# Sending the last quarter's stack rows from the middle of their section, and planning one weight chunk's loads four units later

## The chip, the cores and the metric

The kernel runs on one core of a Trainium2 chip. The core has five engines with a program each: PE (TensorE: matmuls, and its weight loads, shown as PEld), DVE (VectorE), ACT (ScalarE), POOL (GpSimd) and SP (SyncE, which here only issues DMAs). An engine works through its own program in order; engines wait for each other, and for DMAs, on semaphores. The metric is the device time of one execution in microseconds (us), lower is better.

## The reference

The sequence has 2048 rows of 512 numbers. A gate `g` (a sigmoid of a weighted row sum) mixes two results: a two-dimensional Fourier transform written as matrix products, and softmax attention with 32 heads of 16 dimensions.

```python
x = A_x
g = _sigmoid((x * gate_w).sum(-1, keepdims=True))
a = _A_ref(x, ...)     # Real((Cr + i*Ci) @ (x @ Dre.T + i * x @ Dim.T))
...
scores = jnp.einsum("bhqd,bhkd->bhqk", q, k) * scale
p = _softmax(scores, axis=-1)
o = jnp.einsum("bhqk,bhkd->bhqd", p, v)
return g * a + (1 - g) * b     # b = o @ wo
```

Everything is fp32. Products that need it are made from a rounded high part and a low part of each operand (three matmuls instead of one).

## The kernel before

**Attention.** The heads are taken as 16 pairs. The work on the values is cut in 512 *units*, 32 for each pair; `valued` counts the units done. In a unit PE makes score tiles (line 738: a stack `ks` of the keys times a stack `qs` of the queries, 128 keys x 512 queries), ACT takes their exponentials into `pt` (line 739), and PE multiplies `pt` by the values `vt` (line 774, for the last 16 units line 755). In the last 16 units (496 to 511, all of the last pair) the work goes by quarters of 512 queries: units 496 to 503 are the third quarter, 504 to 511 the last.

**Maxima and stack rows.** The exponent needs each query's maximum subtracted. So for every pair, ahead of its scores, PE makes the scores a second time with queries on the partitions (`a_tile`, line 223) and DVE takes their maxima into `mx` (line 225). When a block of queries is through, two functions are put on a list, `deferred`. The first, `m_parts`, folds and negates the maxima on DVE (line 236, `nm`) and splits them into a high and a low part on POOL (lines 239 and 240, `nhl`). The second, `m_rows`, transposes these on DVE (line 244, `mt`) and sends them by eight small DMAs (line 248) into two rows of each head's query stack `qs`: four issued by SP for the first head of the pair, four by POOL for the second. These are the *stack rows*. A score of line 738 reads them as two further rows of its contraction, so it can't start before they are there. For the last pair's second half a block is a quarter, 512 queries.

**What sets the order.** The order is written out. `segment` goes through a pattern of slots: "s" is a score, "a" a tile for the maxima, and each is set beside one matmul of a chain on the other half of the array (line 429; here the product of the attention's output with `wo`). "d" is such a matmul alone. "^" runs one function of `deferred` if there is one. "|" ends the section: first `run_plan` runs what is planned for that unit, then `values` takes two units. One further function of `deferred` is run behind the "|". Each section of the last stretch is named below by its `valued`, 496, 498, 500 and so on, and has its own pair of units behind its scores; scores run two units or more ahead of the values, so the last quarter's first scores stand in section 502.

**The plan.** `at(u, f)` enters a function for unit u; `run_plan` runs all that stand up to `valued + 1`, in order of u and then of entry. For unit 500 stand, in this order: `inverse` for the last four pairs of the first half of the queries (line 534: reciprocal of the softmax sums `rc` on DVE; line 539: two DMAs to `r` in DRAM), `last_block` step 0 (lines 552 and 553: four loads into `o_raw` of 256 KB each, the unscaled output and the reciprocals spread over the rows), and `load_w15` (line 649: eight loads of 64 KB, the chunk of `wo` for the last pair). Step 1 of `last_block` (unit 503, line 587) multiplies the two on POOL, step 2 (unit 505, lines 575 and 576) splits the product on DVE into `o_l`. The chunk w15 is read by the last pair's own products (line 691), first in section 510.

**The end of a quarter.** `LastPair` turns a quarter's finished sum: `copy` (line 666), `turn` (line 672: PE adds and transposes; lines 674 and 676: DVE divides by the sums), `back` (line 682), `products` (line 691). `finish` (line 609) adds a chain's result into an output row block `yp` on DVE; chains use PSUM banks that the scores use too, so a late `finish` or `turn` holds up the next score in that bank.

A DMA that SP issues also waits, if need be, until an earlier DMA with the same semaphore has landed; eight semaphores go round.

Of the kernel before, what the change touches and what calls it, by code (L numbers as in the profile page):

```python
# [32 lines left out]
def mix_kernel(ctx: ExitStack, tc: tile.TileContext, xa_t, xa, wqkv, w_hid, w_seq, wo, gate_w, out):  # L33
# [577 lines left out]
    def proj(hf, cts, pools, qts=range(8), whole=True):  # L611

        for n, qt in enumerate(qts):
            t = hf * 8 + qt
            chain = Chain(pools[n % len(pools)], 3 * len(cts))
            for ct in cts:
                h1, l1 = oh[hf, ct][qt]
                for i, (st, mv) in enumerate(((h1, 0), (h1, 1), (l1, 0))):
                    last = ct == cts[-1] and i == 2
                    yield chain, st, wos[0][:, mv, ct], partial(proj_next, hf, cts, t, chain, whole) if last else None  # L620
# [177 lines left out]
    def take(gen, n, whole=True):  # L798

        got = []  # L800
        while len(got) < n:
            x = next(gen, None)
            if x is None:
                break
            x[0].left -= 1
            got.append((*x, x[0].left == 0))
            if whole and got[-1][4]:
                break
        return got
# [24 lines left out]
    def at(u, f, *args):  # L834
        plan.setdefault(u, []).append(partial(f, *args))
# [19 lines left out]
        at(u, last_block, step, 1, 3, nc.gpsimd)  # L855
    for step, u in enumerate((500, 503, 505)):
        at(u, last_block, step, 0, 4, nc.gpsimd)
    at(500, load_w15)
    lead = a_next

    def run_plan(u):
# [47 lines left out]
    def segment(pattern, half, ds, stop, between=None, hold=True):  # L909


        nonlocal now
        nonlocal users
        before, users = users, []
        ds, late = iter(ds), []
        back = late if hold else None
        for n, slot in enumerate(pattern.split()):
            if slot == "|":
                for f in late:
                    f()  # L920
                add_sums()
                run_plan(valued)
                if between:
                    between()
                values()
                continue
            if slot == "^":
                if deferred:
                    deferred.pop(0)()
                continue  # L930
            now += 1
            ahead = pattern == FULL and 0 < n < 15
            if ahead:
                score(slot[0], 1 - half)
            if len(slot) == 1:
                x = next(ds, None)
                if x:

                    before = before if x[0].begun else None
                    i = issue(x, half, stop, back)  # L940
                    users = []
                    if before:
                        tc.add_manual_dep(
                            i.ins, dict(before[::-1]).get("s", before[0][1]).ins.name,
                            mybir.DependencyInfo(mybir.DependencyClass.Sync, mybir.DependencyReason.DATA))
                        before = None
            if not ahead and slot != "d":
                score(slot[0], 1 - half)
            if len(slot) == 2:
                score(slot[1].lower(), half)  # L950
        if deferred:
            deferred.pop(0)()
# [40 lines left out]
    for hf, qts in ((1, range(2)), (1, range(2, 5)), (1, range(5, 8)), (0, range(2))):  # L993
        for half in range(2):
            ds = take(proj(hf, (3,), [held_bank] * (len(qts) - 1) + one, qts, half == 1), 9, False)
            if valued < UNITS - 12:
                pattern = TEN[half]
            else:
                pattern = "s s s s s s s s |" if len(qts) < 3 else "s s s s d s s s s |"
                if valued == UNITS - 2:  # L1000
                    pattern = "s s s s d d |"
            segment(pattern, half, ds, True, after.get(valued), False)
# [38 lines left out]
```

## Time and profile before

| what | us |
|---|---|
| median of 3 runs (1694.8 to 1695.85) | 1694.96 |
| the profiled execution | 1694.88 |
| its span, first to last instruction | 1693.1 |
| PE busy in it | 1672.5 (99%) |
| DVE, ACT, POOL busy | 1375.7, 1246.4, 751.0 |
| chain that ended last: share of PE | 97% |

The profile of one execution gives the busy time of each engine, the waits (who waited for whom: total, times, longest), the chain of work that ended last, followed back from the end, a timeline of instructions with start and duration, and for any stretch the busy times and the TensorE clock that was granted, as a share of full speed. Times within the span count from its first instruction. PE is busy nearly all of the time, so what can be won lies in the few stretches in which it isn't.

### The profile page before, as it was taken

How to read it: one execution, taken by the hardware profiler on the slowest of the kernel's cores; microseconds unless marked ns; L12 is line 12 of the kernel's file. 1: busy time of each engine (PE TensorE's matmuls, PEld its weight loads, DVE VectorE, ACT ScalarE, POOL GpSimd, SP SyncE). 2: the span in 40 equal slices, each digit the busy share in tenths (PEclk: the TensorE clock that was granted, in tenths of full speed). 3: DMA queues.
4: the chain of work that ended last, by engine and by line, in shares of the span. 5: the costliest groups of instructions: out<-in, count | busy, mean ns of one | idle time of the engine just before them, and what ended most of it. 6: DMA issues, size and time to landing. Idle time of an engine off the chain costs nothing.

```text
span 1693.1 us, 34606 instructions
## 1 busy us (share of the span) xinstructions
PE 1672.5 (99%) x13120; PEld 1016.5 (60%) x13120; DVE 1375.7 (81%) x2295; ACT 1246.4 (74%) x2471; POOL 751.0 (44%) x814
## 2 busy tenths in 40 slices
PE   9999999999999999999999999999999999999987
PEld 7888766655555555555555555555555555555543
DVE  5448688888888888888888888888888888889864
ACT  5212288887777788788877887887787888888874
POOL 0114634554444465454444565545544565222331
PEclk9999999999999999999999999999999999999998
DMA  9963501314141533314164534342231636540122
GB/s 301 332 151 119 170 8 23 44 56 76 38 83 46 102 102 82 73 43 88 45 145 175 115 108 97 80 76 63 70 71 45 128 98 154 218 70 8 36 58 105
DMA packets 82622, 165.16 MB, mean 98 GB/s; under 512 B 19904, under 2 KB 20168, under 8 KB 78616
## 3 DMA queue, kind: packets, MB, share of 16 engines
q1 hardware_dynamic: 77832, 162.30, 37.0%
q8 instruction: 103, 1.69, 0.5%
q0 software_dynamic: 4480, 0.39, 0.3%
q14 instruction: 63, 0.52, 0.1%
q10 hardware_dynamic: 144, 0.26, 0.0%
HBM read 107.73 MB, written 54.52 MB: 96 GB/s over the span
## 4 chain that ended last, share of the span: by engine, by line
PE 97%; DMA 1%; DVE 1%; POOL 1%; issue 0%; SPq 0%; ACT 0%; DVEq 0%; POOLq 0%; ACTq 0%
PE d L429 39%; PE t L774 27%; PE t L223 12%; PE t L738 7%; PE t L318 4%; PE t L90 2%; PE t L91 2%; PE t L89 2%; PE t L336 1%; PE t L755 1%; PE t L429 1%; DVE mx L225 0%; DMA w<-wo 0%; DMA raw<-wqkv 0%; POOL hl L295 0%
## 5 line engine op out<-in xcount | busy, mean ns | idle before, releaser
L225 DVE TENSOR_REDUCE mx<-t 128x1 f32<-128x512 f32 x2022 | 1254.9, 683 | 211.2 <-PE t L223 171.6
L739 ACT ACTIVATE pt<-t 128x512 f32<-128x512 f32 x2048 | 1034.2, 629 | 23.4 <-PE t L738 12.9
L738 PE MATMUL t<-qs,ks 50*128 50x512 f32 x2048 | 741.8, 410 | 11.3 <-DMA qs<-mt 10.7
L223 PE MATMUL t<-ks,qs 48*128 48x512 f32 x2022 | 690.3, 400 | 0.1
L429 PE MATMUL d<-xab,ch 64*128 64x512 f32 x2016 | 656.8, 400 | 0.0
L774 PE MATMUL t<-pt,vt 128*32 128x512 f32 x3968 | 477.1, 598 | 0.2
L429 PEld LDWEIGHTS d<-xab,ch 64*128 64x128 f32 x2016 | 357.8, 184 | 132.5 <-issue 98.9
L738 PEld LDWEIGHTS t<-qs,ks 50*128 50x128 f32 x2048 | 371.1, 185 | 78.1 <-DVE mx L225 38.0
L223 PEld LDWEIGHTS t<-ks,qs 48*128 48x128 f32 x2022 | 367.7, 186 | 80.7 <-ACT pt L739 41.2
L429 PE MATMUL d<-xab,cl 64*128 64x512 f32 x1008 | 403.7, 400 | 0.0
L789 POOL TENSOR_TENSOR osum<-osum,oe 128x512 f32<-128x512 f32 x217 | 279.3, 1287 | 161.8 <-ACT oe L783 159.1
L783 ACT COPY oe<-t 128x512 f32<-128x512 f32 x217 | 127.5, 588 | 230.7 <-PE t L774 228.2
L774 PEld LDWEIGHTS t<-pt,vt 128*32 128x32 f32 x3968 | 103.9, 109 | 231.0 <-issue 148.4
L374 POOL CAST ch<-craw 128x512 fp32r<-128x512 f32 x126 | 77.3, 613 | 351.1 <-PE t L738 300.4
L429 PEld LDWEIGHTS d<-xab,cl 64*128 64x128 f32 x1008 | 185.7, 184 | 67.6 <-issue 51.1
L375 POOL TENSOR_TENSOR cl<-craw,ch 128x512 fp32r<-128x512 f32 x126 | 162.4, 1288 | 10.2
L248 POOL DMA_DIRECT2D qs<-mt x132 | 74.1, 567 | 82.2 <-DVE mt L244 77.2
L429 PE MATMUL d<-wo_hl,o_hl 64*128 64x512 f32 x288 | 77.4, 395 | 0.0
L429 PE MATMUL d<-wre,xab 64*128 64x512 f32 x288 | 70.4, 389 | 0.0
L429 PEld LDWEIGHTS d<-wo_hl,o_hl 64*128 64x128 f32 x288 | 52.2, 185 | 14.0 <-DVE yp L609 5.0
L429 PEld LDWEIGHTS d<-wre,xab 64*128 64x128 f32 x288 | 52.9, 185 | 4.1 <-DVE mx L225 0.3
L90 PE MATMUL t<-xab,wh 128*128 128x512 f32 x128 | 49.9, 390 | 0.2 <-DVE xab L86 0.2
(121 smaller groups left out, 915.4 us busy)
## 6 DMA issues: line engine op xcount, KB each, us to landing
craw<-w_seq SPq DMA_DIRECT2D x128, 256.0 KB
qk<-hl SPq DMA_DIRECT2D x32, 512.0 KB
qs<-qk SPq DMA_DIRECT2D x96, 128.0 KB
ks<-qk SPq DMA_DIRECT2D x96, 128.0 KB
b<-hl SPq DMA_DIRECT2D x16, 512.0 KB
xab<-b SPq DMA_DIRECT2D x16, 512.0 KB
o<-osum SPq DMA_DIRECT2D x62, 128.0 KB
oh<-nh SPq DMA_DIRECT2D x12, 512.0 KB
```

What stands on the lines that cost most here:

```text
L90: nc.tensor.matmul(ps, sh, ml, start=False, stop=False)
L223: nc.tensor.matmul(ps, qs[p % 2][r, qt * P:(qt + 1) * P], ks[p % 2][r, kb * 512:(kb + 1) * 512], start=True, stop=True)
L225: user = nc.vector.tensor_reduce(mx[p % 2][:, h, qt, kb:kb + 1], ps, AX.X, ALU.max)
L248: (nc.sync, nc.gpsimd)[h].dma_start(rows.rearrange("v (q b c) -> v b q c", q=n, b=4)[:, b], mt[k % 2][32 * b + h:32 * b + 4 * n:2])
L374: nc.gpsimd.tensor_copy(h1, raw)
L375: nc.gpsimd.tensor_tensor(l1, raw, h1.bitcast(F32), ALU.subtract)
L429: i = nc.tensor.matmul(self.ps, st[r], mv[r], start=not self.begun, stop=stop)
L738: nc.tensor.matmul(ps, ks[p % 2][rr, kt * P:(kt + 1) * P], qs[p % 2][rr, q0:q0 + 512], start=True, stop=True)
L739: return nc.scalar.activation(pts[u][:, 2 * qb + h], ps, AF.Exp, bias=0.0, scale=DH ** -0.5)
L774: nc.tensor.matmul(acc[32 * j:32 * j + 32], vt[:, kt, p, h:h + 32], pt[:, j], start=u == us[0], stop=u == us[-1])
L783: nc.scalar.copy(oe, acc)
L789: nc.gpsimd.tensor_tensor(o, o, oe, ALU.add)
```

## The change

Two lines differ. The sections from `valued` 500 on get a "^" behind their second score, which runs one function of `deferred` there rather than behind the section's end. And `load_w15` is entered for unit 504 instead of 500.

```diff
     for step, u in enumerate((500, 503, 505)):
         at(u, last_block, step, 0, 4, nc.gpsimd)
-    at(500, load_w15)
+    at(504, load_w15)
...
             else:
-                pattern = "s s s s s s s s |" if len(qts) < 3 else "s s s s d s s s s |"
+                pattern = "s s ^ s s s s s s |" if len(qts) < 3 else "s s ^ s s d s s s s |"
                 if valued == UNITS - 2:
                     pattern = "s s s s d d |"
```

Only one function is on the list in these sections: `m_rows` of the last quarter, in section 500. On DVE, this is the piece of the program in that section, before (-) and with the change (+); `nhl` is what POOL split, the three line 609 are the section's finishes, line 534 is the reciprocal of `inverse`:

```order
 L236 TENSOR_REDUCE nm_170<-mx_168 128x2x4
+L244 STREAM_TRANSPOSE mt_174<-nhl_172 128x32
 L609 SCALAR_TENSOR_TENSOR yp_20655<-t,omg,yp_20655 128x512
 L609 SCALAR_TENSOR_TENSOR yp_20656<-t,omg,yp_20656 128x512
 L609 SCALAR_TENSOR_TENSOR yp_20657<-d,omg,yp_20657 128x512
 L534 RECIPROCAL rc<-rc 128x64
-L244 STREAM_TRANSPOSE mt_174<-nhl_172 128x32
 L609 SCALAR_TENSOR_TENSOR yp_20655<-t,omg,yp_20655 128x512
```

The transpose has moved ahead of three finishes and the reciprocal; nothing else on DVE has moved.

On SP, the program at the same place before the change; `w` is the chunk w15, line 528 loads the softmax sums, line 627 is the first output row block:

```order
 L528 DMA rc<-o_104 64x1x64 x2
 L539 DMA r_151<-rc 16x4x64 x2
 L552 DMA o_raw<-o_104 64x1x1024
 L553 DMA o_raw<-r_151 64x1x1024
 L552 DMA o_raw<-o_104 64x1x1024
 L553 DMA o_raw<-r_151 64x1x1024
 L649 DMA w_23186<-wo_141 16x1024 x8
 L248 DMA qs_935<-mt_174 2x4x32 x4
 L627 DMA out<-yp_21644 128x512
```

And with the change:

```order
 L528 DMA rc<-o_104 64x1x64 x2
 L248 DMA qs_935<-mt_174 2x4x32 x4
 L539 DMA r_151<-rc 16x4x64 x2
 L552 DMA o_raw<-o_104 64x1x1024
 L553 DMA o_raw<-r_151 64x1x1024
 L552 DMA o_raw<-o_104 64x1x1024
 L553 DMA o_raw<-r_151 64x1x1024
 L649 DMA w_23295<-wo_141 16x1024 x8
 L627 DMA out<-yp_21644 128x512
```

The four row DMAs have moved from behind the chunk's loads to ahead of everything of `inverse` and `last_block`. The chunk's loads still stand right behind those of `o_raw` and ahead of the first output: SP has nothing else to issue between units 500 and 504.

The orders of PE, ACT and POOL are the same in both programs. One unchanged place matters below, at the change from section 504 to 506. On DVE, at the end of section 504, with the semaphores that each row waits for; `o_raw` and `o_l` are those of `last_block`, `t_23307` is the PSUM tile of `turn`:

```order
 L609 SCALAR_TENSOR_TENSOR yp15_20723<-d_23289,omg_166,yp15_20723 128x512 [waits PE_49]
 L575 CAST o_l_23304<-o_raw_22715 128x1024 [waits DMAHW7_49,DMAHW5_49,Pool_49]
 L576 TENSOR_TENSOR o_l_23304<-o_raw_22715,o_l_23304 128x1024 [waits DVE_49]
 L674 RECIPROCAL rc15_23075<-t_23307 128x8 [waits PE_49]
 L676 TENSOR_TENSOR on15_23074<-t_23307,rc15_23075 128x4x16 [waits DVE_49]
```

And on PE, in section 506, where the score `t_23344` takes over the bank of `t_23307` and therefore waits for DVE:

```order
 L429 MATMUL t_23328<-wo_hl_20347,o_lnh_22939 128x512
 L738 MATMUL t_23339<-qs1_935,ks1_937 128x512 [waits Activation_49]
 L429 MATMUL t_23342<-wo_hl_20347,o_lnh_22939 128x512 [waits Activation_49]
 L738 MATMUL t_23344<-qs1_935,ks1_937 128x512 [waits DVE_49,PE_49]
 L429 MATMUL t_23342<-wo_hl_20347,o_lnh_22939 128x512 x2
```

Neither has moved: line 676, which reads `t_23307` last, stands behind lines 575 and 576, and line 575 waits for POOL's product of line 587.

## Prediction

> **What bounds the kernel now.** I read the page first (busy time, share of the span, instructions): PE is the bound throughout, so the question is where PE stands still in the stretch that the change touches, the last 60 us.
>
> ```profile
> PE 1672.5 (99%) x13120; PEld 1016.5 (60%) x13120; DVE 1375.7 (81%) x2295; ACT 1246.4 (74%) x2471; POOL 751.0 (44%) x814
> ```
>
> The waits of the stretch from 1560 us name one long PE wait, for the stack rows (`qs<-mt`), and with it a wait of ACT of the same length (total, times, longest).
>
> ```profile
> PE t L738 <- DMA qs<-mt: 10.7, 2, 10.5
> ACT pt L739 <- PE d L429: 10.3, 1, 10.3
> ```
>
> The chain of work that ended last (start, length, what) tells why the rows are late:
>
> ```profile
> 1641.84 0.54 DVE rc L534
> 1642.46 0.49 SPq L539
> ...
> 1646.18 5.11 DMA w<-wo
> 1651.39 0.70 SPq L248
> ...
> 1653.51 1.61 DMA qs<-mt
> 1655.26 0.76 PE t L738
> ```
>
> SP issues in order. Ahead of the rows stand the reciprocals, the loads of `o_raw` and the eight loads of w15. The eight take 5.11 us, because in the program the last four of them wait for semaphores that the `o_raw` loads hold until they land. The rows themselves need 3.87 us from their first issue (1651.39) to the first score (1655.26). The same stretch by stages (length, then PE, PEld, DVE, ACT, POOL busy, granted clock, DMA):
>
> ```profile
> 1636.81:1641.28 4.47, 4.47 (x35) 2.19 (x34) 2.44 (x5) 4.02 (x10) 0.39 (x2) 1.00 0.00 0
> 1644.80:1655.26 10.46, 0.00 (x1) 0.03 (x2) 0.78 (x2) 0.94 (x2) 2.48 (x2) 0.64 0.62 151
> 1655.26:1661.37 6.11, 6.11 (x26) 2.28 (x27) 1.11 (x2) 2.06 (x4) 0.00 (x0) 0.50 0.00 1
> ```
>
> PE is idle for 10.46 us and then works for 6.11 us at half clock: the stall is paid twice. A mean of 0.64 over 10.46 us is full clock for 2.9 us and half for the rest, so it took 2.9 us without work until the clock fell.
>
> **The rows, moved to the middle of section 500.** What matters is when they land now. The timeline of DVE, POOL and SP there (start, duration, what, idle before):
>
> ```profile
> 1637.64 0.19 DVE L236 TENSOR_REDUCE nm<-mx 128x8 f32<-128x32 f32 x1
> 1639.66 1.45 DVE L609 SCALAR_TENSOR_TENSOR yp<-t,omg,yp 128x512 f32<-128x512 f32 x2 [1.83 <-PE t L738]
> 1642.30 0.15 DVE L244 STREAM_TRANSPOSE mt<-nhl 128x32 f32<-128x32 f32 x1
> 1638.17 0.20 POOL L240 TENSOR_TENSOR nhl<-nm,nhl 128x8 fp32r<-128x8 f32 x1
> 1642.75 2.19 POOL L248 DMA_DIRECT2D qs<-mt  x4 [4.38 <-DVE mt L244]
> 1651.05 2.33 POOL L587 TENSOR_TENSOR o_raw<-o_raw 128x1024 f32<-128x1024 f32 x1 [6.11 <-DMA o_raw<-r]
> 1642.41 1.19 SPq L539 DMA_DIRECT2D r<-rc  x2
> 1651.39 2.73 SPq L248 DMA_DIRECT2D qs<-mt  x4
> ```
>
> POOL has the parts ready at 1638.37, and DVE is idle for 1.83 us ahead of the finishes at 1639.66. The transpose (0.15) fits into that gap and delays no finish; without the gap it would cost its 0.15. It ends at about 1638.7; with the 0.30 us that lie between its end and POOL's first issue before (1642.45 to 1642.75), both queues start issuing at 1639.0. SP is through at 1639.0 + 2.73 = 1641.7, before it needs to issue the reciprocals (1642.41): 0.7 us of cover, beyond which each us delays r, `o_raw` and line 587 by as much. With the 3.87 us of before, SP's rows are there at 1642.9. POOL's four issues start 3.75 us earlier too and end at 1641.2; nothing stands behind them on POOL until 1651.05, and the first score that waits for them is the next section's.
>
> PE reaches the score when? The section ahead has the same row order, at full clock (PE, start and duration):
>
> ```profile
> 1636.81 1.92 PE L755 MATMUL t<-pt,vt 128*32 128x512 f32 x16
> 1638.66 0.49 PE L429 MATMUL t<-wo_hl,o_lno 64*128 64x512 f32 x1
> 1639.00 0.39 PE L429 MATMUL t<-wo_hl,o_lno 64*128 64x512 f32 x1
> 1639.88 0.50 PE L738 MATMUL t<-qs,ks 50*128 50x512 f32 x1
> 1639.93 0.39 PE L429 MATMUL t<-wo_hl,o_lno 64*128 64x512 f32 x1
> 1641.28 1.06 PE L755 MATMUL t<-pt,vt 128*32 128x512 f32 x8
> 1643.94 0.86 PE L429 MATMUL t<-wo_hl,o_lno 64*128 64x512 f32 x3
> 1657.23 3.64 PE L755 MATMUL t<-pt,vt 128*32 128x512 f32 x16
> 1660.80 0.73 PE L429 MATMUL t<-wo_hl,o_lnh 64*128 64x512 f32 x1
> 1661.37 0.40 PE L429 MATMUL t<-wo_hl,o_lnh 64*128 64x512 f32 x1
> ```
>
> There the score (1639.88) starts beside the third line 429 (1639.93). In the stalled section the third of the three from 1643.94 starts at 1643.94 + 0.86 - 0.39 = 1644.4. So rows that land at 1642.9 are 1.5 us early.
>
> Terms, at most: the wait, start to start, 1655.26 - 1644.4 = 10.9; the half clock: score to values 1.97 (1655.26 to 1657.23) against 1.40 (1639.88 to 1641.28), values 3.57 against 1.85, first pair 0.57 against 0.34, together 6.11 against 3.59, 2.5. That is 13.4. At least, with the wait as the profile counts it (10.46), 13.0. I take 13.2, between the two; ACT, busy 4.02 of 4.47 us in a section at full clock, keeps that pace.
>
> **What is late next.** The product of line 587 does not move: the reciprocals are still issued at 1642.41, `o_raw` and w15 behind them as before, so it still runs from 1651.05 to 1653.38. Before, DVE came to its split (line 575) at 1664.12, long after. With 13.2 us less it comes at 1650.9 and must wait.
>
> ```profile
> 1664.44 1.93 PE L755 MATMUL t<-pt,vt 128*32 128x512 f32 x16
> 1664.12 0.68 DVE L575 CAST o_l<-o_raw 128x1024 fp32r<-128x1024 f32 x1
> 1664.84 1.23 DVE L576 TENSOR_TENSOR o_l<-o_raw,o_l 128x1024 fp32r<-128x1024 f32 x1
> 1666.21 0.36 DVE L676 TENSOR_TENSOR on<-t,rc 128x64 f32<-128x64 f32 x2
> 1667.12 0.39 PE L738 MATMUL t<-qs,ks 50*128 50x512 f32 x1
> ```
>
> From the start of line 575 to the end of line 676 are 1666.57 - 1664.12 = 2.45 us. Started at 1653.45, just behind POOL, they end at 1655.9. PE's score `t_23344`, the row at 1667.12, comes up at 1667.12 - 13.2 = 1653.9 and now waits 2.0 us, with some 0.1 for the semaphore 2.1. Everything behind it on PE moves by that: the rest of the kernel is a row of PE work to the end, and its outputs follow PE. Bounds of this term: 0, if the `o_raw` loads land 2 us sooner, and 4.1, if they land 2 us later; nothing that moves shares much with them (eight row DMAs, few bytes), so I keep 2.1.
>
> **w15 planned for unit 504.** In the issue order its loads stay directly behind `o_raw`, and an issue waits for no engine's place in the plan; nothing gained or lost: 0. Without the "^" it would have let the rows pass the loads; with it, they are past already. It is read first at line 691, tens of us behind its landing.
>
> **Sum.** 13.2 - 2.1 = 11.1 us off the profiled execution's 1694.88 gives 1683.8. The median of before is 0.08 above that execution, which I neglect. The 0.2% that separate a change from none are 3.4 us.
>
> [...] POOL's row DMAs now run beside DVE's three finishes. All of POOL's and SP's row issues of the kernel:
>
> ```profile
> L248 POOL DMA_DIRECT2D qs<-mt x132: 544/561/637, 173.9 to 1644.4; - x132
> L248 SPq DMA_DIRECT2D qs<-mt x132: 599/618/799, 174.4 to 1653.5; - x132
> DMA to landing us min/median/max: 1.6/1.7/4.9
> ```
>
> POOL's 132 issues took 544 to 637 ns, in a kernel where DVE is busy for 81% of the span: none was held. [...]
>
> [...] The wait of 2.1 us that I expect at `t_23344` is shorter than the 2.9 us without work after which the clock fell here. [...]
>
> **The rivals.** *No second wait* (0.12): `o_raw` lands early enough or line 676 isn't waited for. 1694.9 - 13.2 = 1681.7. For it: one PSUM bank alone links the two. Against: line 587's start is fixed by transfers that don't move.
>
> *The rows come late* (0.10): their DMAs take longer than before. At the longest landing of the kernel, 4.9 us, the fourth issue (1639.0 + 3 x 0.62 = 1640.9) lands at 1645.8, 1.4 us after PE wants it: 1685.2, less what this takes off the second wait. Against: the median is 1.7, and the DMA engines are idle at that time.
>
> *The second wait halves the clock too* (0.06): it costs what half clock cost before, 2.5 us: 1686.3.
>
> *POOL's issue is held by DVE* (0.02): if its four issues could only start when the finishes and the reciprocal are done (1641.84 + 0.54 = 1642.4) they end 2.19 later, at 1644.6. The next section's first pair needs the rows at about 1647.6 (1645.8 and 1.85 for the values). With the median landing of 1.7 us they are there; with the longest, 4.9, they are 1.9 late, 1685.7 at most.
>
> *Slower* (0.03): the transpose, in its new place, holds what stands behind it. If its input from POOL came late, DVE's finishes would wait, then the reciprocal, SP's r and `o_raw` behind it, and PE at the banks of the finishes: us for us from 1639.2. At the moment when PE got its rows before, 1655.3, that would be 1683.8 + 16.1 = 1699.9; slower than before from 1650.3 on. Against: POOL has nothing ahead of lines 239 and 240 in that section, and they ended at 1638.37.
>
> *The change does nothing* (0.01): the rows wait on SP for something else than its order, and land as before: 1694.9.
>
> **How the numbers follow.** The forecast case has 0.66: 1683.8, give or take 1 for the two terms. The range reaches from the case without a second wait, less 0.4 for the larger first term (1681.3), to the case with the clock (1686.6). Faster by over 0.2%: all but the last two, 0.96; the same 0.01; slower 0.03.
>
> **What the profile of the changed kernel would show.** The transpose (line 244) between line 236 and the finishes at 1639.66, SP's line 248 starting near 1639.0, no PE wait on `qs<-mt`, granted clock 1.00 through 1645 to 1661, values of section 502 near 1645.8 and of 504 near 1651.2. Line 587 still near 1651.05, line 575 just behind it at 1653.4, and a PE wait of about 2 us for DVE near 1654. Wrong would be the forecast if `o_raw`'s loads shift against 1651, if PE waits longer than 2.9 us there, or if the score waits on a row DMA after all.

## The result, and the profile after

| | median us (lowest to highest) |
|---|---|
| before, runs beside the changed kernel's | 1695.39 (1694.80 to 1695.85, 4 executions) |
| changed | 1685.20 (1684.79 to 1685.77, 4 executions) |
| ratio | 0.994, 95% interval 0.9923 to 0.9958 |

The change saves 10.2 us, 0.6%. The forecast was 1683.8, so 11.1 us; the measured median lies 1.4 us above it and inside the range. The profiled execution took 1684.99, with a span of 1683.2.

The page shows that PE is the bound as before; its busy time is about the same (1670.9 against 1672.5), in a span that is 9.9 us shorter.

```profile
PE 1670.9 (99%) x13120; PEld 1014.2 (60%) x13120; DVE 1376.7 (82%) x2295; ACT 1246.9 (74%) x2471; POOL 751.0 (45%) x814
```

Among the waits from 1560 us on (total, times, longest), PE's wait for the stack rows has gone from 10.7 us to 0.3, and that one lies ahead of 1636, where nothing changed. In its place stands a row of three that hang together: POOL waits for the loads of `o_raw`, DVE for POOL, PE for DVE.

```profile
POOL o_raw L587 <- DMA o_raw<-r: 10.2, 1, 10.2
DVE o_l L575 <- POOL o_raw L587: 3.0, 1, 3.0
PE t L738 <- DVE on L676: 2.3, 1, 2.3
PE t L738 <- DMA qs<-mt: 0.3, 1, 0.3
```

**The offset.** This trace as a whole lies 1.14 us later than that of before by the time it gets to the changed stretch: line 755 of section 500 starts at 1642.42 against 1641.28. The 1.14 is there already at line 755 of section 498 (1637.95 against 1636.81), which stands ahead of the transpose (1639.54) and of all else that the change moves, and the other executions below, of the same program too, have offsets from 0.03 to 0.58 at section 500. So the offset belongs to the execution, not to the change, and where a time of after is set against one of before I take 1.14 off it ("aligned").

The timeline of DVE, SP and POOL (start, duration, what, idle before) shows the moved step. The transpose (line 244) runs at 1639.54, right behind POOL's parts and ahead of the finishes; both queues then issue the rows.

```profile
1638.79 0.19 DVE L236 TENSOR_REDUCE nm<-mx 128x8 f32<-128x32 f32 x1
1639.54 0.21 DVE L244 STREAM_TRANSPOSE mt<-nhl 128x32 f32<-128x32 f32 x1 [0.57 <-POOL nhl L240]
1639.78 2.73 SPq L248 DMA_DIRECT2D qs<-mt  x4
1640.05 2.19 POOL L248 DMA_DIRECT2D qs<-mt  x4 [0.55 <-DVE mt L244]
1640.80 1.45 DVE L609 SCALAR_TENSOR_TENSOR yp<-t,omg,yp 128x512 f32<-128x512 f32 x2 [1.05 <-PE t L738]
1643.55 1.21 SPq L539 DMA_DIRECT2D r<-rc  x2
```

On PE, the score that stalled before (1645.47) stands in its row without a wait. The values of sections 502 and 504 follow at full speed; then the score `t_23344` waits.

```profile
1642.42 1.92 PE L755 MATMUL t<-pt,vt 128*32 128x512 f32 x16
1645.47 0.49 PE L738 MATMUL t<-qs,ks 50*128 50x512 f32 x1
1646.87 1.92 PE L755 MATMUL t<-pt,vt 128*32 128x512 f32 x16
1652.13 1.92 PE L755 MATMUL t<-pt,vt 128*32 128x512 f32 x16
1657.45 0.47 PE L738 MATMUL t<-qs,ks 50*128 50x512 f32 x1 [2.27 <-DVE on L676]
1659.30 1.92 PE L755 MATMUL t<-pt,vt 128*32 128x512 f32 x16
```

The chain of work that ended last used to pass through the row DMAs (line 248). Now it passes from SP's loads over POOL and DVE to that score (start, length, what):

```profile
1642.98 0.55 DVE rc L534
1643.55 0.57 SPq L539
...
1646.75 5.53 DMA o_raw<-r
1652.44 2.38 POOL o_raw L587
1654.85 0.70 DVE o_l L575
1655.58 1.23 DVE o_l L576
1656.95 0.37 DVE on L676 x2
1657.45 0.47 PE t L738
```

By stages (length, then PE, PEld, DVE, ACT, POOL busy, granted clock, DMA) PE is busy throughout where it was idle before, and in this execution the clock stays at 1.00, also behind the new wait:

```profile
1645.70:1651.20 5.50, 5.50 (x43) 2.85 (x40) 3.94 (x7) 5.05 (x11) 0.00 (x0) 1.00 0.91 214
1656.50:1658.30 1.80, 0.84 (x8) 0.82 (x10) 1.50 (x6) 0.34 (x1) 0.00 (x0) 1.00 0.00 0
1658.30:1662.00 3.70, 3.55 (x31) 1.43 (x29) 1.67 (x3) 2.65 (x7) 0.00 (x0) 1.00 0.02 4
```

Aligned, the kernel ends at 1683.2 - 1.14 = 1682.06 against 1693.1: the changed stretch gained 11.04 us.

### The profile page after: what moved, and what is told of

It reads as the page before. It is cut to its first block, busy times and chain, and to the rows that moved or that the text cites. A ratio compares the mean times of both kernels' runs of the same rounds, so it can differ in the third digit from the quotient of the medians.

```text
span 1683.2 us, 34607 instructions
## 1 busy us (share of the span) xinstructions
PE 1670.9 (99%) x13120; PEld 1014.2 (60%) x13120; DVE 1376.7 (82%) x2295; ACT 1246.9 (74%) x2471; POOL 751.0 (45%) x814
## 4 chain that ended last, share of the span: by engine, by line
PE 97%; DVE 1%; POOL 1%; DMA 1%; issue 0%; SPq 0%; ACT 0%; DVEq 0%; POOLq 0%; ACTq 0%
PE d L429 39%; PE t L774 27%; PE t L223 11%; PE t L738 7%; PE t L318 4%; PE t L89 2%; PE t L90 2%; PE t L91 2%; PE t L336 1%; PE t L755 1%; PE t L429 0%; DVE mx L225 0%; DMA o_raw<-r 0%; PE t L160 0%; POOL hl L295 0%
## 5 line engine op out<-in xcount | busy, mean ns | idle before, releaser
L375 POOL TENSOR_TENSOR cl<-craw,ch 128x512 fp32r<-128x512 f32 x126 | 162.3, 1288 | 10.2
```

Source lines behind the costliest of these rows:

```text
L375: nc.gpsimd.tensor_tensor(l1, raw, h1.bitcast(F32), ALU.subtract)
```

## The experiments

My theory: the "^" alone makes the gain; the plan of w15 does nothing beside it; the second wait is set by DVE's split (lines 575, 576), which stands ahead of line 676 and waits for POOL; and that in turn is set by the `o_raw` loads. The rivals: the two edits only work together; w15's loads share in how late `o_raw` lands; something else than the split holds line 676; and what the forecast missed is the clock behind the new wait. All kernels compute the whole reference.

### The "^" alone

The changed kernel with w15 planned for unit 500 as before.

```diff
-    at(504, load_w15)
+    at(500, load_w15)
```

> Only the "^" of the change; the chunk w15 stays planned for unit 500. Theory (SP's issue order sets when the rows land, the plan of w15 has no part in it): SP's order is that of the changed kernel row for row, so the time is the changed kernel's, 1685.2 give or take 0.5. Rival (the later plan of w15 gave a part of the gain, since the loads of w15 shared the DMA engines with the rows): slower than the changed kernel by 1 us or more, at most the 10 us of the gain.

Measured: 1685.41 (1683.78 to 1686.15), ratio 0.9941 (0.9927 to 0.9954). That is the changed kernel's time, as the programs are the same row for row: the plan's edit does nothing once the "^" is there. But this profiled execution shows what the one above does not. PE waits 2.58 us at the same score (timeline: start, duration, what, idle before),

```profile
1656.90 0.46 PE L738 MATMUL t<-qs,ks 50*128 50x512 f32 x1 [2.58 <-DVE on L676]
1658.96 3.06 PE L755 MATMUL t<-pt,vt 128*32 128x512 f32 x16
```

and then the clock falls, to 0.60 on average over this stage:

```profile
1658.30:1662.00 3.70, 3.70 (x21) 0.83 (x19) 1.17 (x3) 1.81 (x5) 0.00 (x0) 0.60 0.02 4
```

The sixteen values of section 506 take 3.06 us instead of 1.92.

### The plan of w15 alone

The changed kernel without the "^". The rows then stand on SP behind the `o_raw` loads but ahead of w15's.

```diff
-                pattern = "s s ^ s s s s s s |" if len(qts) < 3 else "s s ^ s s d s s s s |"
+                pattern = "s s s s s s s s |" if len(qts) < 3 else "s s s s d s s s s |"
```

> Only the later plan of w15; no "^". The rows now stand on SP behind the loads of o_raw but ahead of those of w15, and the transpose is where it was before. Theory: SP issues the rows from about 1646.1 instead of 1651.4, 5.3 us sooner, so PE waits some 5.6 us, from 1644.4 to 1650.0; that is longer than 2.9 us, so the clock still halves and its 2.5 us are still paid, and there is no second wait, since DVE reaches line 575 near 1659. 1695.4 - 5.3 = 1690.1. If the clock didn't halve it would be 1687.6. Rival (the transfers of o_raw, not the order of issue, hold the rows): the rows land only when o_raw has landed, after 1651, and the gain is under 4 us, 1691.5 or more.

Measured: 1690.78 (1689.95 to 1692.08, 7 executions), ratio 0.9975 (0.9965 to 0.9986), 4.3 us below the 1695.1 of before in those runs. The rows are issued at 1646.78 instead of 1651.39, but PE waits for them still (timeline):

```profile
1646.78 2.72 SPq L248 DMA_DIRECT2D qs<-mt  x4
1652.33 0.76 PE L738 MATMUL t<-qs,ks 50*128 50x512 f32 x1 [6.95 <-DMA qs<-mt]
1661.41 0.68 DVE L575 CAST o_l<-o_raw 128x1024 fp32r<-128x1024 f32 x1
```

The stage behind it runs at half clock, as it did before:

```profile
1652.33:1658.44 6.11, 6.11 (x25) 2.27 (x27) 1.12 (x2) 2.06 (x4) 1.80 (x1) 0.50 0.21 55
```

From the first issue to the score are 1652.33 - 1646.78 = 5.55 us, against 3.87 before: with a megabyte of `o_raw` still on its way, the rows take 1.68 us longer. That is more than the 1.0 us by which the median gained less than the theory's 5.3; the profiled execution is the slowest of the seven (1692.08). So w15's place in SP's order cost a part (this run takes that away), and the large loads around the rows another (only the "^" takes the rows away from them). Which loads these are is not shown. The packets of the four row DMAs (128 bytes each) start to move at 1650.22, 3.44 us behind the first issue (1.34 before), but their last has moved by 1650.57, and the last DMA lands only at 1652.19, 3.30 us after its issue (1.61 before). By then w15's loads, which SP issues right behind the rows, from 1649.54 on, are moving too. There is no second wait here: DVE comes to its split only at 1661.41, and its row shows no idle time ahead.

### The split two units later

The changed kernel with step 2 of `last_block` (lines 575 and 576) planned for unit 507. On DVE it then stands behind line 676 instead of ahead of it.

```diff
-    for step, u in enumerate((500, 503, 505)):
+    for step, u in enumerate((500, 503, 507)):
```

> The changed kernel, with step 2 of the last block (lines 575 and 576) planned for unit 507 instead of 505: on DVE it moves behind lines 674 and 676 and the next section's three finishes. Theory (the wait of PE for line 676 behind line 575 is what is left on the path): that wait of 2.6 us goes. The split is then wanted by line 429 in section 508, about 0.5 to 1 us before it is done, so 1.6 to 2.1 us of the 2.6 are gained: 1683.3 give or take 0.5. Rival (something else is as late as this wait, such as the scores' pace on ACT): no faster than 1684.7.

Measured: 1681.55 (1681.35 to 1682.00), ratio 0.992 (0.9906 to 0.9933). This beats both kernels: 13.5 us below before, 3.65 below the changed one, and the highest of its executions lies below the lowest of the changed kernel's, 1683.78 over the 13 executions of its program here. It also lies below the 1683.3, give or take 0.5, that I expected: line 429 of section 508 was to wait 0.5 to 1 us for the split, and the profile lists no wait of PE from 1640 us on. The wait for line 676 is gone, as the timeline of POOL, DVE and PE shows:

```profile
1651.19 2.37 POOL L587 TENSOR_TENSOR o_raw<-o_raw 128x1024 f32<-128x1024 f32 x1 [9.82 <-DMA o_raw<-r]
1651.60 0.36 DVE L676 TENSOR_TENSOR on<-t,rc 128x64 f32<-128x64 f32 x2
1655.98 1.92 PE L755 MATMUL t<-pt,vt 128*32 128x512 f32 x16
1656.29 0.68 DVE L575 CAST o_l<-o_raw 128x1024 fp32r<-128x1024 f32 x1
```

POOL's product is no earlier, but line 676 no longer stands behind it: it runs at 1651.60 instead of 1656.95 (aligned 1651.34 instead of 1655.81). The split comes at 1656.29, when its input has been there for 2.7 us. So it was the order on DVE that made the second wait. The gain over the changed kernel is more than the 2.1 that the prediction had put on the wait: the wait was longer, and where the clock halved behind it, that goes too.

### w15's loads ahead of the rows

The changed kernel with w15 planned for unit 498. SP issues its loads from 1634.98 on, when nothing else is to be issued, so they no longer follow or overlap the `o_raw` loads.

```diff
-    at(504, load_w15)
+    at(498, load_w15)
```

> The changed kernel, with the loads of w15 planned for unit 498: on SP they now stand ahead of the rows, in time in which SP had nothing to issue (1635 to 1639), and off the DMA engines when o_raw is loaded. Theory (line 587 is late because the 0.5 MB of w15 share the DMA engines with the 1 MB of o_raw): o_raw lands about 2 us sooner, near 1648.8 to 1649.3 instead of 1651.2, line 575 waits little or not, and the wait of PE of 2.6 us shrinks to under 0.7. The rows are issued about 0.8 us later, 1639.8, and land at 1643.7, still ahead of 1644.4. 1683.0 give or take 0.6. Rival (o_raw's landing is set by its own loads, four times 256 KB behind the reciprocals): line 587 starts where it did and the time stays 1685.2.

Measured: 1685.41 (1683.36 to 1687.44, 5 executions), ratio 0.9939 (0.9926 to 0.9953). No gain: that theory fell. Its timeline:

```profile
1651.47 2.38 POOL L587 TENSOR_TENSOR o_raw<-o_raw 128x1024 f32<-128x1024 f32 x1 [10.34 <-DMA o_raw<-r]
1656.49 0.46 PE L738 MATMUL t<-qs,ks 50*128 50x512 f32 x1 [2.42 <-DVE on L676]
1658.32 3.52 PE L755 MATMUL t<-pt,vt 128*32 128x512 f32 x16
```

POOL's product starts at 1651.47 (offset 0.03), no earlier than with w15 behind (aligned: 1651.30 in after). The `o_raw` loads take as long by themselves; w15's cost them nothing. In this execution, too, the clock halved behind the wait: values of 3.52 us.

### The "^" four slots later

The transpose then stands behind the section's second finish instead of ahead of the first. This spends the margin that the rows had.

```diff
-                pattern = "s s ^ s s s s s s |" if len(qts) < 3 else "s s ^ s s d s s s s |"
+                pattern = "s s ^ s s s s s s |" if len(qts) < 3 else "s s s s d s ^ s s s |"
```

> The changed kernel with the "^" four slots later in its section: on DVE the transpose stands behind two of the three finishes (near 1641.1 instead of 1638.6), on SP the rows are still ahead of the reciprocals, issued from about 1641.6. Theory (the place in the middle matters for two reasons: the score wants the rows at 1644.4, and SP must be through with them by 1642.4): the rows land 1.1 us late and PE waits that long; the reciprocals are issued near 1644.4, 2.0 us late, and with them o_raw, line 587 and line 575, on which PE waits in the next section but one. The later of the two decides: 2.0 us slower than the changed kernel, 1687.2 give or take 0.7. Rival (SP's cover of 0.7 us doesn't matter, only the rows do): 1.1 us slower, of which the second wait gives back as much: 1685.2 to 1686.3.

Measured: 1687.08 (1686.42 to 1688.31), ratio 0.9954 (0.9939 to 0.9969); 1.9 above the changed kernel. The timeline of SP, PE and POOL:

```profile
1641.48 2.73 SPq L248 DMA_DIRECT2D qs<-mt  x4
1644.31 1.20 SPq L539 DMA_DIRECT2D r<-rc  x2
1645.35 0.47 PE L738 MATMUL t<-qs,ks 50*128 50x512 f32 x1 [0.32 <-DMA qs<-mt]
1653.16 2.37 POOL L587 TENSOR_TENSOR o_raw<-o_raw 128x1024 f32<-128x1024 f32 x1 [9.21 <-DMA o_raw<-r]
1658.17 0.76 PE L738 MATMUL t<-qs,ks 50*128 50x512 f32 x1 [3.43 <-DVE on L676]
```

The two stages behind that last wait:

```profile
1658.30:1662.00 3.70, 3.70 (x19) 1.98 (x23) 2.17 (x4) 2.72 (x6) 0.00 (x0) 0.50 0.02 4
1662.00:1666.00 4.00, 4.00 (x28) 1.48 (x20) 0.54 (x2) 0.97 (x2) 0.00 (x0) 0.72 0.00 0
```

The rows take 1645.35 - 1641.48 = 3.87 us from first issue to score, to the hundredth what they took before, and hold PE for only 0.32 us. What costs is SP's queue: the rows now push the reciprocals (line 539) back on SP, by about 1.6 us (1644.31 against 1642.70 in the repeated run below), and with them `o_raw`, POOL's product and the split, so the second wait is 3.43 us and the clock is at half through the next stretch and for over half of the one after (0.50 over 3.70 us, 0.72 over 4.00). This is the cover of SP that the prediction had put at 0.7 us; in the repeated run it is 1.0, from the end of the row issues at 1641.67 to 1642.70.

### The split later, without the change

Before, with step 2 of `last_block` at unit 507.

```diff
-    for step, u in enumerate((500, 503, 505)):
+    for step, u in enumerate((500, 503, 507)):
```

> The kernel before, with step 2 of the last block planned for unit 507 as in the version that gained 3.6 us on the changed kernel. Theory (the wait behind line 575 came only with the change: before, line 587 was done 11 us ahead of DVE): no difference, 1695.1 give or take 0.6. Rival (the later split is worth something by itself, as DVE's 1.9 us stood ahead of the turn): 1694.0 or less.

Measured: 1694.79 (1693.96 to 1695.46, 10 executions), ratio 1.0 (0.9991 to 1.0009). No difference, as expected: in the kernel before, the split's place was free, because PE stood waiting for the rows while POOL finished (timeline of its profile):

```profile
1655.40 0.76 PE L738 MATMUL t<-qs,ks 50*128 50x512 f32 x1 [10.19 <-DMA qs<-mt]
```

The second wait belongs to the change.

### The changed kernel again

No edit. The question is whether the half clock that two other kernels showed is theirs or the changed kernel's.

> The changed kernel once more, for the spread of its times. Theory (the second wait of about 2.5 us halves the clock for one window of 3.4 us in some executions and in others not): times from 1683.8 to 1686.5 as in the version with the "^" alone, wider than the version without that wait (1681.4 to 1682.0); the profiled execution has either no half clock before 1675, or one of 3.4 us just behind the wait. Rival (the clock doesn't answer to this wait): all within 0.6 us and no half clock.

Measured: 1685.29 (1683.92 to 1687.41, 5 executions), ratio 0.9946 (0.9933 to 0.9958). Timeline and, below it, the stage behind the wait:

```profile
1642.70 1.20 SPq L539 DMA_DIRECT2D r<-rc  x2
1656.51 0.47 PE L738 MATMUL t<-qs,ks 50*128 50x512 f32 x1 [2.17 <-DVE on L676]
1658.36 3.55 PE L755 MATMUL t<-pt,vt 128*32 128x512 f32 x16
```

```profile
1658.30:1662.00 3.70, 3.70 (x19) 0.77 (x20) 0.72 (x2) 1.42 (x4) 0.00 (x0) 0.54 0.02 4
```

It is the changed kernel's. The times reach higher than the 1686.5 expected; what made one execution take 1687.41 is not known. Here the wait is 2.17 us, shorter than the 2.27 of the first profiled execution, and yet the clock falls 1.8 us behind its end. A mean of 0.54 over 3.70 us is half clock for 0.46 / 0.5 x 3.70 = 3.4 us. All profiled executions beside each other (the offset by line 755 of section 500; the end less the offset, against 1693.1):

| profiled execution | offset | PE's wait for line 676 | clock behind it | values of 506 | aligned end |
|---|---|---|---|---|---|
| after | 1.14 | 2.27 | full | 1.92 | -11.04 |
| the same again | 0.30 | 2.17 | half | 3.55 | -9.50 |
| "^" alone | 0.28 | 2.58 | half | 3.06 | -9.38 |
| w15 ahead of the rows | 0.03 | 2.42 | half | 3.52 | -9.23 |
| "^" four slots later | 0.23 | 3.43 | half | 3.52 | -6.83 |
| split later | 0.26 | none | full | 1.92 | -13.46 |

The first three rows are the same program. With the half clock it gains some 1.6 us less.

## Why the prediction was right, and where it was off

**The rows, moved.** Right, in place and size. The transpose fitted into DVE's gap, SP began to issue at 1639.78 (aligned 1638.64; forecast 1639.0), and SP's cover held, as line 539 starts just behind the reciprocal. The stalled score stands at 1645.47, aligned 1644.33 (1644.4). Section 504's values begin at 1652.13, aligned 1650.99, where before they began at 1664.44: 13.45 us for a term put at 13.2, and just above its bounds of 13.0 and 13.4. The run with the split later is the same term by itself, without the second: its end is 13.46 us earlier. The 3.87 us of the rows were measured again with the "^" four slots later; by them the rows were there at 1639.78 + 3.87 = 1643.65, 1.8 us ahead of the score.

**What is late next.** Right in kind, with its chain link by link, and a little small. POOL's product starts at 1652.44 (aligned 1651.30, forecast 1651.05 as before), the split at 1654.85 (aligned 1653.71, forecast 1653.45), and PE's score at 1657.45, aligned 1656.31. Without the wait it would have come at 1667.12 - 13.45 = 1653.67, so the wait costs 2.6 us from start to start, 2.27 as the profile counts it; I had 2.1. The 0.25 us of POOL's later start and the 0.25 of the larger first term make up the difference. The 0.1 that I had put in for the semaphore, by no row shown, was 0.13: line 676 ends at 1656.95 + 0.37 = 1657.32, and the score starts at 1657.45. The reason given, that `o_raw`'s loads do not move, holds, and w15 ahead of the rows shows that w15 has no part in how late they are. POOL's start differs by itself from one execution to the next: 1651.61 with the "^" alone and 1651.19 in the repeat, each less its offset, of the same program.

**The plan of w15.** Right: nothing, as the "^" alone shows. By itself it would have been worth 4.3 us.

**The clock behind the second wait.** This is the step that failed. I put it at 0.06, on the ground that "the wait of 2.1 us that I expect at `t_23344` is shorter than the 2.9 us without work after which the clock fell here". The 2.9 us were one event, and I made a threshold of it. The same program halved its clock behind waits of 2.17 and 2.58 us and did not behind one of 2.27. The price was too high as well: 1.6 us in these executions, not 2.5, since 3.4 us at half clock fall on PE's work here, against 6.1 behind the stall of before.

How long the clock was at half follows from its mean in the stages, as worked out for the repeat: 3.4 us there (0.99 over 1.80 us, then 0.54 over 3.70), with the "^" alone (0.88 and 0.60 over the same stages) and with w15 ahead of the rows (1.00 and 0.54); 6.8 with the "^" four slots later (0.76 and 0.50, then 0.72 over 4.00); 10.3 with the plan of w15 alone (0.73 over the 6.83 us up to the score, 0.50 over 6.11, 0.93 over 3.26). In the trace of before it was 13.65, from 1647.67 to 1661.32. In these runs the lengths lie near one, two, three and four times 3.4 us.

The falls fit no single time without work: they came 2.7 us behind the start of the wait with the "^" four slots later, 2.9 in before, 3.3 with the plan of w15 alone, 3.55 with the "^" alone and 3.9 in the repeat. Nor does PE's work just ahead tell the outcomes apart. Below are the 3.41 us (a quarter of the 13.65 of before) of after that end with its wait, and those of the repeat that end with the fall (1658.27, by the 0.99 over 1.80 us):

```profile
1654.04:1657.45 3.41, 1.14 (x10) 0.64 (x8) 2.53 (x6) 1.57 (x3) 0.78 (x1) 1.00 0.00 0
1654.86:1658.27 3.41, 1.62 (x11) 1.10 (x11) 3.12 (x7) 1.69 (x4) 0.00 (x0) 1.00 0.00 0
```

After has the longer wait and less PE work in its stretch, 1.14 us against 1.62, and yet its clock stays at 1.00 there and, as the stages show, up to 1662. What decides between two executions of one program is not shown.

**Sum.** In the profiled execution the changed stretch gained 11.04 us for 11.1 forecast; its time of 1684.99 is above 1683.8 by the offset of 1.14, which is the execution's. The median is above the forecast by 1.4 us. Half clock in part of the executions, at 1.6, and offsets could account for that size, but how often the clock halves in executions without a profile was not measured: only two of the three profiled ones showed it. Held to the likeliest case alone, the forecast should have had the half clock in it: 13.2 - 2.1 - 1.6 = 9.5 off gives 1685.4. The forecast case by itself, 1683.8 give or take 1, ends at 1684.8; the median lies inside the range because the range reaches to the case with the half clock, which had been given 0.06. That much is luck.

**The other rivals.** *No second wait* was wrong, and the split later shows what it would have been worth: 1681.55, forecast for that rival 1681.7. *The rows come late* did not happen; they had 1.8 us to spare. *POOL's issue held by DVE* did not happen: the four issues took 2.19 us in a row beside the finishes, as before, and all 132 of POOL 544 to 637 ns each, in both traces. *Slower* and *nothing* fell with the result.

## What to carry to other kernels

When a long stall is taken away, look for work that only fitted behind it: here a step of DVE whose place in the order cost nothing while PE stood still (no difference without the change) cost 3.65 us once PE did not, and moving it two units later cost nothing either. A small DMA that PE waits for belongs ahead of large loads on its queue, both for the order of issue (the plan of w15 alone, which took the rows past eight loads, gained 4.3 us) and for the transfers in flight around it (5.55 us from first issue to score there, 3.87 with the "^" four slots later). A PE wait of some 2 us was not safe from the clock here (half behind 2.17 and 2.58 us, full behind 2.27); count a possible stretch at half clock with it, some 3.4 us long and worth 1.6 in this program, rather than take one threshold from one event.

## What the runs showed of the hardware

That the clock can halve behind a wait as short as 2.17 us, and stay full behind one of 2.27 us of the same program, was new to me; what tells the two apart was not shown. So was what four small DMAs lose among large ones: with the plan of w15 alone they took 5.55 us from first issue to use, behind a megabyte of `o_raw` loads and just ahead of those of w15. They took 3.87 us with the "^" four slots later, and also before, where only the last w15 loads were left ahead of them. How little that was, a stretch of before shows that begins just ahead of the rows' issue (stages as above, the last two columns the DMA engines' share and GB/s):

```profile
1651.20:1656.50 5.30, 1.24 (x6) 1.14 (x7) 0.00 (x0) 0.44 (x1) 2.18 (x1) 0.50 0.10 26
```

26 GB/s over 5.30 us are 0.14 MB, about two loads of 64 KB. Whether the small DMAs wait for the large ones' packets or share with them was not told apart.
